# A one-token decode block on one Trainium2 core: how the output weight wo is laid out, loaded and multiplied at the end

## The chip, the cores and the metric

The kernel runs on one core of a Trainium2 chip. The metric is the time on the device of one execution in microseconds (us); the number of the kernel before is the median of ten executions. The profile is of one further execution with the hardware profiler on.

## The reference, cut to what matters

One token of width 512 is normalised and goes through an attention over a long cache and, beside it, a small two-layer network; both are added to the token.

```python
xn = _layernorm(x)                                  # x: (1, 1, 512), bfloat16
q = (xn @ wq) -> 32 heads of 128                    # wq: 512 x 4096
k, v = k_cache, v_cache, each head used by 4 q heads    # (1, 8, 65536, 128)
p = softmax(q k^T * 128 ** -0.5)
o = p v                                             # 32 heads of 128
A = o.reshape(1, 1, 4096) @ wo                      # wo: 4096 x 512
B = gelu(xn @ w1 + b1) @ w2 + b2                    # w1: 512 x 1792
return x + A + B
```

The cache is two times 134 MB, so nearly all of the 280 MB that are read are K and V. The weight wo has 4 MB; its row 128 h + d belongs to element d of head h.

## The kernel before, in words

**Tiling.** Eight groups (G) of four query heads (HPG) share a K and V head each. The 65,536 keys of a group are cut into four chunks, so there are 32 units of 16,384 keys. Two units make a pair, and `body(i)` works through pair i, 16 times. All of K, V and the weights of the first stage go through one SBUF tile, `kv`, of four slots of 4 MB (32 KB in each of 128 partitions): slots 0 and 1 take the K of even and odd units, slots 2 and 3 together the V of a pair.

**A body.** For each unit, `transposes` turns 128 x 128 blocks of K on TensorE (L585) into PSUM, VectorE and ScalarE copy them to `kt_ring` (L593, L595), and `scores` multiplies them by q (L605). `stats_1` and `stats_2` find the maximum and take exponentials; `pv` multiplies them by V (L676), 128 matmuls per unit, and VectorE keeps the result in `o_all` (L685). In the last body `weigh_1`, `weigh_2` and `weigh_3(0, GE, "oT")` weigh the chunks of the first seven groups (GE = 7) together into `oT_all`, which has d on partitions and one column per head; `weigh_3(GE, G, "oL")` does it for the last group after the last `pv`.

**What sets the order.** Each engine runs its own list, written out by hand. `_Sched.op` and `_Sched.dma` note what each step reads and writes and put semaphore waits where another engine or a DMA is to be waited for. All large loads are issued by SP, in the order of the list `chunks`: K of two units, V of the pair, and so on, at the end "W", which calls `dma_wo`. `issue_chunks` runs this list as slots come free; SP itself waits in that order, for a K slot till its transposes are done, for a V slot till its `pv` is done. When a pair of V has landed, GpSimd writes a one-element `flag` (L437), and the `pv` of the odd unit waits for that. PE, VectorE and ScalarE run the first 15 bodies or all 16 as a rolled loop.

**The end.** `dma_wo` loads wo for groups 0 to 3 and 4 to 6 in two DMAs of 4 KB rows into slot 0 (L469): for each group, partition p holds the four wo rows 4p to 4p + 3. The four heads of the last group go to slot 1 in 1 KB rows (L478): three heads in one DMA, the fourth in one of 120 partitions and one of 8. Since a partition of the first seven groups holds four neighbouring rows, the attention outputs must be moved to fit: sixteen small matmuls with columns of the identity (L774) pick them from `oT_all` into PSUM, and VectorE copies them to `oX_bf` (L778). Then `fin_mm` (L786) accumulates into one PSUM bank: 4 matmuls for the other branch and the bias (8 in the trace, as they are float32), 112 for the first seven groups, 16 for the last. VectorE copies the sum to `fin_bf` (L801), and SP writes it out (L805).

## Time and profile before

| | |
|---|---|
| median of ten executions | 659.0 us (658.77 to 659.18) |
| the profiled execution | 659.36 us |
| its span, first to last instruction | 657.6 us |
| mean TensorE clock granted | 0.768 of full speed |
| busy share: PE, DVE, ACT, POOL | 82%, 42%, 37%, 0% |
| read from HBM | 280.50 MB, 427 GB/s over the span |
| SP's queue | 9119 packets, 280.50 MB, 99.2% of 16 engines' span |
| instruction fetches (queue q8) | 8 packets, 0.13 MB |
| issue of the first wo load to its landing | 24.3 us for 2048 KB |
| issue of the second | 27.9 us for 1536 KB |
| three heads of the last group | 18.0 us for 384 KB |

How to read it: PE is TensorE, DVE VectorE, ACT ScalarE, POOL GpSimd; SP is the engine that only issues DMAs. A busy share is an average over the span; a wait for a DMA in it may be short and still set the end. The time from issue to landing of a load includes its time in the queue behind the loads issued earlier. The DMA share is that of the core's sixteen DMA engines, and the trace also keeps a record of each packet (a contiguous piece that one DMA engine moves): its start, its length, its bytes and its queue, though not its engine.

### The profile page before, as it was taken

What the parts mean: (1) busy time and instruction counts of PE and PEld (TensorE: products, weight loads), DVE (VectorE), ACT (ScalarE), POOL (GpSimd) and SP (SyncE); (2) the same over time, 40 slices, a digit from 0 to 9 for tenths busy, and PEclk for the clock granted to TensorE, in tenths of its full rate; (3) what the DMA queues carried; (4) which work ended last, traced back from release to release, by engine and by line L of the source; (5) the groups of instructions that cost most, each with busy time, mean ns of one, the idle gap of its engine ahead of it and who ended that gap; (6) DMA issues with size and microseconds to landing.
All of it is one profiled execution on the core that took longest, in us unless ns stands there. A gap on an engine that the chain in (4) does not pass through costs nothing.

```text
span 657.6 us, 27984 instructions
## 1 busy us (share of the span) xinstructions
PE 537.2 (82%) x12695; PEld 510.3 (78%) x12695; DVE 273.6 (42%) x565; ACT 245.0 (37%) x454; POOL 2.9 (0%) x27
## 2 busy tenths in 40 slices
PE   1388699988789697878969787895978879697897
PEld 0187698978788697868959787895978779597886
DVE  3145172725436162453516345261634526154352
ACT  0134162524425152352505335160443516144351
POOL 0000000000000000000000000000000000000000
PEclk9788596967869597786958778595877959588695
DMA  8999999999999999999999999999999999999997
GB/s 365 437 440 431 420 435 429 441 425 460 411 443 427 425 464 397 448 425 448 443 403 439 425 464 403 439 439 423 462 401 441 425 439 456 407 439 425 435 427 274
DMA packets 9277, 280.65 MB, mean 427 GB/s; under 512 B 1073, under 2 KB 1587, under 8 KB 2483
## 3 DMA queue, kind: packets, MB, share of 16 engines
q1 hardware_dynamic: 9119, 280.50, 99.2%
q8 instruction: 8, 0.13, 0.1%
q10 hardware_dynamic: 148, 0.01, 0.0%
q14 instruction: 2, 0.02, 0.0%
HBM read 280.50 MB, written 0.00 MB: 427 GB/s over the span
## 4 chain that ended last, share of the span: by engine, by line
DMA 65%; PE 32%; issue 2%; DVE 0%; SPq 0%
DMA kv<-in_A_k_cache_dram 61%; PE pst L585 25%; DMA kv<-in_A_wo_dram 4%; PE pss L605 4%; PE pO L676 2%; PE pA L632 0%; PE pss L786 0%; PE pA L643 0%; DVE pmax L613 0%; PE pA L692 0%; DVE gmax L634 0%; DVE diag L636 0%; SPq L460 0%; SPq L453 0%; SPq L457 0%
## 5 line engine op out<-in xcount | busy, mean ns | idle before, releaser
L595 ACT ACTIVATE kt_ring<-pst 128x1024 bf16<-128x1024 bf16 x192 | 195.6, 1027 | 311.1 <-PE pst L585 309.7
L585 PE MATMUL pst<-ident_bf,kv 128*128 128x128 bf16 x4096 | 282.1, 235 | 35.2 <-DMA kv<-in_A_k_cache_dram 35.1
L585 PEld LDWEIGHTS pst<-ident_bf,kv 128*128 128x128 bf16 x4096 | 263.8, 107 | 43.4 <-DMA kv<-in_A_k_cache_dram 36.6
L593 DVE COPY kt_ring<-pst 128x1024 bf16<-128x1024 bf16 x320 | 210.7, 687 | 121.6 <-PE pst L585 119.2
L676 PE MATMUL pO<-P_bf,kv 128*128 128x4 bf16 x4096 | 115.1, 166 | 38.5 <-DMA kv<-in_A_v_cache_dram 32.8
L676 PEld LDWEIGHTS pO<-P_bf,kv 128*128 128x128 bf16 x4096 | 113.6, 104 | 39.9 <-DMA kv<-in_A_v_cache_dram 34.0
L605 PE MATMUL pss<-q_cur,kt_ring 128*128 128x4 bf16 x4096 | 111.9, 164 | 3.8 <-issue 3.8
L605 PEld LDWEIGHTS pss<-q_cur,kt_ring 128*128 128x128 bf16 x4096 | 109.3, 96 | 3.9 <-issue 3.9
L654 ACT ACTIVATE P_bf<-pss,negm 128x128 bf16<-128x128 f32 x128 | 50.9, 548 | 67.5 <-DVE negm L646 67.5
L685 DVE COPY o_all<-pO 128x4 f32 (+1 forms) x32 | 5.2, 162 | 122.4 <-PE pO L676 122.4
L613 DVE TENSOR_REDUCE pmax<-pss 128x4 f32<-128x512 f32 x32 | 22.1, 692 | 67.6 <-PE pss L605 67.6
L654 ACT ACTIVATION_READ_ACCUMULATOR P_bf<-pss,negm 128x1 f32 x128 | 35.4, 277 | 0.0
L643 PEld LDWEIGHTS pA<-diag,ones_f 4*128 4x128 f32 x64 | 12.6, 245 | 18.2 <-DVE diag L636 16.5
L632 PE MATMUL pA<-ident_f,pmax 128*4 128x128 f32 x64 | 14.3, 312 | 12.5 <-DVE pmax L613 12.5
L643 PE MATMUL pA<-diag,ones_f 4*128 4x4 f32 x64 | 15.4, 309 | 10.0 <-DVE diag L636 10.0
L632 PEld LDWEIGHTS pA<-ident_f,pmax 128*4 128x4 f32 x64 | 2.9, 84 | 15.7 <-DVE pmax L613 14.0
L634 DVE TENSOR_REDUCE gmax<-pA 4x1 f32<-4x128 f32 x32 | 8.8, 274 | 9.5 <-PE pA L632 9.5
L668 DVE COPY sums_all<-sums 128x8 f32 (+1 forms) x16 | 2.7, 171 | 23.4 <-ACT P_bf L654 23.4
L692 PE MATMUL pA<-sums_all,ones_f 128*128 128x128 f32 x32 | 12.4, 491 | 0.0
L646 DVE TENSOR_SCALAR negm<-pA 128x4 f32<-128x4 f32 x32 | 5.1, 161 | 10.8 <-PE pA L643 10.8
L692 PEld LDWEIGHTS pA<-sums_all,ones_f 128*128 128x128 f32 x32 | 8.0, 312 | 0.0
L520 PE MATMUL pss<-kv,xnT_bf 128*1 128x512 bf16 x32 | 3.6, 627 | 4.8 <-DMA kv<-in_A_wq_dram 4.8
(75 smaller groups left out, 50.3 us busy)
## 6 DMA issues: line engine op xcount, KB each, us to landing
kv<-in_A_k_cache_dram SPq DMA_DIRECT2D x32, 4096.0 KB, 27.5
kv<-in_A_v_cache_dram SPq DMA_DIRECT2D x4, 4096.0 KB, 23.8
kv<-in_A_wq_dram SPq DMA_DIRECT2D x1, 4096.0 KB, 12.6
kv<-in_B_w_dram SPq DMA_DIRECT2D x2, 1792.0 KB, 18.3
kv<-in_A_wo_dram SPq DMA_DIRECT2D x1, 2048.0 KB, 24.3
kv<-in_A_wo_dram SPq DMA_DIRECT2D x1, 1536.0 KB, 27.9
kv<-in_A_wo_dram SPq DMA_DIRECT2D x1, 384.0 KB, 18.0
kv<-in_A_v_cache_dram SPq DMA_DIRECT2D x14, 31.1
```

Source lines behind the costliest of these rows:

```text
L585: lambda tb=tb, at=at, b=b, tt=s * TPB + t: pe.transpose(pst[tb][:, at * 128:(at + 1) * 128], slot[b][:, tt, :], ident_bf[:, :]),
L593: e, fn = DVE, lambda tb=tb, dst=dst: dve.tensor_copy(out=dst, in_=pst[tb][:, :])
L595: e, fn = ACT, lambda tb=tb, dst=dst: act.activation(out=dst, in_=pst[tb][:, :], func=ACTF.Copy)
L605: lambda k=k, kb=kb, at=at, t=t: pe.matmul(pss[k][:, at:at + HPG], lhsT=kt_ring[:, kb * BCOL + t * 128:kb * BCOL + (t + 1) * 128], rhs=q_c ...
L613: lambda k=k: dve.tensor_reduce(out=pmax[:, :], in_=pss[k][:, 0:CW].rearrange("p (t j) -> p j t", j=HPG), axis=AX.X, op=ALU.max),
L632: sch.op(PE, lambda: pe.matmul(pA[0:HPG, PA_ST:PA_ST + 128], lhsT=pmax[:, 0:HPG], rhs=ident_f[:, :], start=True, stop=True), reads=["pmax" ...
L634: sch.op(DVE, lambda: dve.tensor_reduce(out=gmax4[:, :], in_=pA[0:HPG, PA_ST:PA_ST + 128], axis=AX.X, op=ALU.max), reads=["pA"], writes=[" ...
L643: sch.op(PE, lambda: pe.matmul(pA[:, PA_SB:PA_SB + HPG], lhsT=ones_f[0:HPG, 0:128], rhs=diag4[0:HPG, 0:HPG], start=True, stop=True), reads ...
L654: lambda k=k, at=at, j=j, src=src: act.activation(out=P_v[k][:, :, j], in_=src[:, :, j], func=ACTF.Exp, bias=negm[:, at:at + 1], scale=1.0 ...
L676: lambda k=k, t=t: pe.matmul(pO[:, 0:HPG], lhsT=vslot[:, k * TPD + t, :], rhs=P_v[k][:, t, :], start=t == 0, stop=t == TPD - 1),
L685: sch.op(DVE, lambda: dve.tensor_copy(out=o_all[:, at_pair(i, PW, k * HPG, HPG)], in_=pO[:, 0:HPG]), reads=["pO"], writes=[f"o{k}"])
L692: sch.op(PE, lambda: pe.matmul(pA[:, PA_SUM:PA_SUM + NC], lhsT=ones_f[:, :], rhs=sums_all[:, :], start=True, stop=True), reads=["ones_f", ...
```

## The change

Of wo's first 28 heads (seven groups), what was two DMAs of 4 KB rows becomes three pieces, `WP`: four groups, two groups, one group. In a piece of n groups partition p holds 4n neighbouring rows of wo: 16, 8 and 4 KB. The first piece gets a buffer of its own, `wa`; the others stay in slot 0, and the 8 KB piece has the wait for that slot. The first piece is loaded in three parts. Partitions 0 to 111 are loaded by SP at the end, in place of the first wo load. Partitions 112 to 127 are loaded in sixteen DMAs of one partition from GpSimd's queue, each of 8,179 of the 8,192 elements, and a DMA of 16 x 13 elements by SP; both are placed ahead of body 4 (`dma_rest`), on GpSimd behind the flag of V pair 4. The fourth head of the last group is loaded in one DMA of 128 partitions.

The attention outputs are moved to fit in another way: for each piece, VectorE multiplies the columns of `oT_all`, repeated, by a mask of zeros and ones, `part_m` (`spread`, before the last `pv`), and one matmul with `part_r` sums the right rows. The two masks of each piece come from the identity by a reduction on VectorE ahead of the loop. Three matmuls replace sixteen; the copy to `oX_bf` comes ahead of `weigh_3(GE, G, "oL")`. The number of final matmuls is the same; the 64 of the first piece read `wa`.

```diff
--- before.py
+++ after.py
@@ -332,7 +332,21 @@
     w2_at = w1_at + KT * F
     w2_sb = kv[:, w2_at:w2_at + FC * D].rearrange("p (fc n) -> p fc n", fc=FC)
     GE = G - 1
-    wo_sb = kv[:, 0:GE * HPG * D].rearrange("p (g r n) -> p g r n", g=GE, r=HPG)
+    WP = []
+    g0 = 0
+    while g0 < GE:
+        n = next(m for m in (4, 2, 1) if g0 + m <= GE)
+        WP.append((g0, n))
+        g0 += n
+    NS = 16
+    WA = WP[0][1] * HPG
+    LP = WA * D - 13
+    wa = sb("wa", [128, WA * D], BF)
+    wo_sb = kv[:, WA * D:GE * HPG * D].rearrange("p (r n) -> p r n", n=D)
+
+    def wo_row(r, cols):
+        return wa[:, r * D + cols.start:r * D + cols.stop] if r < WA else wo_sb[:, r - WA, cols]
+
     wl_at = TPD * DH
     wl_sb = kv[:, wl_at:wl_at + HPG * D].rearrange("p (h n) -> p h n", h=HPG)
     kt_ring = sb("kt_ring", [128, NKT * BCOL], BF)
@@ -356,7 +370,10 @@
     rden = sb("rden", [128, H], F32)
     o_sum = sb("o_sum", [128, H], F32)
     oT_all = sb("oT_all", [128, H], BF)
-    oX_bf = sb("oX_bf", [128, HPG, GE], BF)
+    oX_bf = sb("oX_bf", [128, GE * HPG], BF)
+    oM_bf = sb("oM_bf", [128, len(WP), 128], BF)
+    part_m = [sb(f"part_m{i}", [128, DH // (n * HPG)], BF) for i, (_, n) in enumerate(WP)]
+    part_r = [sb(f"part_r{i}", [128, n * HPG], BF) for i, (_, n) in enumerate(WP)]
     flag = sb("flag", [1, 1], F32)
 
     pst = [nc.alloc_psum_tensor(f"pst{i}", [128, 1024], BF) for i in range(NPT)]
@@ -376,7 +393,9 @@
     sem_misc = sch.dsem("dmisc")
     sem_w1 = sch.dsem("dw1")
     sem_w2 = sch.dsem("dw2")
-    wsem = [sch.dsem(f"wsem{i}") for i in range(4)]
+    wsem = [sch.dsem(f"wsem{i}") for i in range(len(WP))]
+    lsem = [sch.dsem(f"lsem{i}") for i in range(2)]
+    sem_wa, sem_wb = sch.dsem("dwa"), sch.dsem("dwb")
     sem_vb = sch.dsem("dvb")
     sem_out = sch.dsem("dout")
 
@@ -460,26 +479,35 @@
         sch.dma(SP, lambda: sp.dma_start(out=w2_sb, in_=B_w2.rearrange("(p fc) n -> p fc n", fc=FC)),
                 sem_w2, writes=["w2"])
 
-    WG = (4, GE - 4)
     WH = (HPG - 1, 1)
 
+    def src_wa():
+        return A_wo[0:WA * DH, :].rearrange("(p r) n -> p (r n)", r=WA)
+
+    def dma_rest():
+        for p in range(128 - NS, 128):
+            sch.dma(POOL, lambda p=p: pool.dma_start(out=wa[p:p + 1, 0:LP], in_=src_wa()[p:p + 1, 0:LP]), sem_wa,
+                    writes=["wo0r"], total=16 * NS)
+        sch.dma(SP, lambda: sp.dma_start(out=wa[128 - NS:128, LP:WA * D],
+                                           in_=src_wa()[128 - NS:128, LP:WA * D]), sem_wb, writes=["wo0s"])
+
     def dma_wo():
-        g0 = 0
-        for i, n in enumerate(WG):
-            sch.dma(SP, lambda g0=g0, n=n: sp.dma_start(
-                out=wo_sb[:, g0:g0 + n].rearrange("p g r n -> p g (r n)"),
-                in_=A_wo[g0 * HPG * DH:(g0 + n) * HPG * DH, :].rearrange("(g p r) n -> p g (r n)", p=128, r=HPG)),
-                wsem[i], writes=[f"wo{i}"] + (["slot0"] if i == 0 else []))
-            g0 += n
+        for i, (g0, n) in enumerate(WP):
+            r = n * HPG
+            if i == 0:
+                sch.dma(SP, lambda: sp.dma_start(out=wa[0:128 - NS, :], in_=src_wa()[0:128 - NS, :]), wsem[i],
+                        writes=["wo0"])
+                continue
+            sch.dma(SP, lambda g0=g0, n=n, r=r: sp.dma_start(
+                out=wo_sb[:, g0 * HPG - WA:g0 * HPG - WA + r, :],
+                in_=A_wo[g0 * HPG * DH:(g0 + n) * HPG * DH, :].rearrange("(p r) n -> p r n", r=r)),
+                wsem[i], writes=[f"wo{i}"] + (["slot0"] if i == 1 else []))
         h0 = 0
         for i, n in enumerate(WH):
-            cuts = ((0, 128),) if n > 1 else ((0, 120), (120, 128))
-            for j, (p0, p1) in enumerate(cuts):
-                sch.dma(SP, lambda h0=h0, n=n, p0=p0, p1=p1: sp.dma_start(
-                    out=wl_sb[p0:p1, h0:h0 + n, :],
-                    in_=A_wo[(H - HPG + h0) * DH:(H - HPG + h0 + n) * DH, :].rearrange(
-                        "(h p) n -> p h n", p=128)[p0:p1, :, :]),
-                    wsem[2 + i], writes=[f"wl{i}"] + (["slot1"] if i == 0 else []), total=16 * len(cuts))
+            sch.dma(SP, lambda h0=h0, n=n: sp.dma_start(
+                out=wl_sb[:, h0:h0 + n, :],
+                in_=A_wo[(H - HPG + h0) * DH:(H - HPG + h0 + n) * DH, :].rearrange("(h p) n -> p h n", p=128)),
+                lsem[i], writes=[f"wl{i}"] + (["slot1"] if i == 0 else []))
             h0 += n
 
     dma_small()
@@ -721,6 +749,16 @@
                reads=["o_sum", "rden"], writes=[res])
 
 
+    def spread():
+        for i, (g0, n) in enumerate(WP):
+            r, a = n * HPG, DH // (n * HPG)
+            sch.op(DVX, lambda g0=g0, n=n, i=i, r=r, a=a: dve.tensor_tensor(
+                out=oM_bf[:, i, :].rearrange("p (h a) -> p h a", a=a),
+                in0=oT_all[:, g0 * HPG:g0 * HPG + r].unsqueeze(2).to_broadcast([128, r, a]),
+                in1=part_m[i][:, :].unsqueeze(1).to_broadcast([128, r, a]), op=ALU.mult),
+                reads=["oT", f"part_m{i}"], writes=[f"oM{i}"])
+
+
     def body(i):
         last = i == NU // 2 - 1
         for b in range(2):
@@ -749,6 +787,7 @@
         if last:
             weigh_2()
             weigh_3(0, GE, "oT")
+            spread()
         pv(2 * i + 1)
 
     for t, res in ((pss[0], "pss0"), (pss[1], "pss1"), (pO, "pO"), (pA, "pA")):
@@ -759,25 +798,30 @@
     ffn()
     free.add("V1")
     done_chunk("V0")
+    for i, (_, n) in enumerate(WP):
+        r = n * HPG
+        for t, res, pat in ((part_m[i], f"part_m{i}", "p (a r) -> p a r"), (part_r[i], f"part_r{i}", "p (a r) -> p r a")):
+            sch.op(DVE, lambda t=t, pat=pat, r=r: dve.tensor_reduce(
+                out=t[:, :], in_=ident_f[:, :].rearrange(pat, r=r), axis=AX.X, op=ALU.max),
+                reads=["ident_f"], writes=[res])
     marks, marks2 = [], []
     for i in range(NU // 2):
         marks.append(len(PE.ops))
         marks2.append((len(DVE.ops), len(ACT.ops)))
         assert not (DVE.pending or ACT.pending)
+        if i == 4:
+            dma_rest()
         body(i)
     marks.append(len(PE.ops))
 
 
+    for i, (g0, n) in enumerate(WP):
+        r = n * HPG
+        sch.op(PE, lambda g0=g0, i=i, r=r: pe.matmul(
+            pA[:, PA_O + g0 * HPG:PA_O + g0 * HPG + r], lhsT=oM_bf[:, i, :], rhs=part_r[i][:, :], start=True, stop=True),
+            reads=[f"oM{i}", f"part_r{i}"], writes=["pA"])
+    sch.op(DVX, lambda: dve.tensor_copy(out=oX_bf[:, :], in_=pA[:, PA_O:PA_O + GE * HPG]), reads=["pA"], writes=["oX"])
     weigh_3(GE, G, "oL")
-    for r in range(HPG):
-        for h in range(HPG):
-            sch.op(PE, lambda r=r, h=h: pe.matmul(
-                pA[32 * h:32 * h + 32, PA_O + r * GE:PA_O + (r + 1) * GE], lhsT=ident_bf[:, r:128:HPG],
-                rhs=oT_all[:, h:GE * HPG:HPG], start=True, stop=True),
-                reads=["oT", "ident_bf"], writes=["pA"], publish=r == HPG - 1 and h == HPG - 1)
-    sch.op(DVX, lambda: dve.tensor_copy(
-        out=oX_bf[:, :, :], in_=pA[:, PA_O:PA_O + HPG * GE].rearrange("p (r g) -> p r g", r=HPG)),
-        reads=["pA"], writes=["oX"])
 
     R = 0
     pR = pss[R]
@@ -788,11 +832,11 @@
 
     for kt in range(KT):
         fin_mm(kt, ones_f[:, 0:1], f_rows[:, kt * 128:(kt + 1) * 128], ["f_rows", "ones_f"], True, False, kt == KT - 1)
-    for g in range(GE):
-        for r in range(HPG):
+    for i, (g0, n) in enumerate(WP):
+        for r in range(g0 * HPG, (g0 + n) * HPG):
             for kt in range(KT):
-                fin_mm(kt, oX_bf[:, r, g:g + 1], wo_sb[:, g, r, kt * 128:(kt + 1) * 128],
-                       ["oX", f"wo{0 if g < WG[0] else 1}"], False, False, r == HPG - 1 and kt == KT - 1)
+                fin_mm(kt, oX_bf[:, r:r + 1], wo_row(r, slice(kt * 128, (kt + 1) * 128)), ["oX", f"wo{i}"] + ["wo0r", "wo0s"] * (i == 0), False, False,
+                       r == (g0 + n) * HPG - 1 and kt == KT - 1)
     for h in range(HPG):
         for kt in range(KT):
             fin_mm(kt, oT_all[:, GE * HPG + h:GE * HPG + h + 1], wl_sb[:, h, kt * 128:(kt + 1) * 128],
```

## The prediction

> **What bounds the kernel now.** I read the DMA share by stage, then the chain of waits in the last 34 us, then the packet records of the trace. The share first. After the clock and before GB/s, each row gives the share of the sixteen DMA engines that is busy.

> ```profile
> 100.00:200.00 100.00, 88.12 (x2155) 85.07 (x2153) 42.02 (x87) 38.81 (x71) 0.27 (x3) 0.76 1.01 434
> 200.00:300.00 100.00, 83.96 (x2011) 80.33 (x2009) 42.21 (x87) 39.20 (x78) 0.29 (x3) 0.77 1.00 432
> ...
> 500.00:600.00 100.00, 86.92 (x2051) 83.55 (x2049) 46.55 (x91) 43.64 (x76) 0.18 (x2) 0.80 1.00 434
> ```

> There is no idle DMA time, while PE is busy 84 to 88 us in 100. GpSimd's flag (L437), set when a pair of V has landed, shows the period: 38.65 to 38.83 us, 15 times. A period moves 16.8 MB, at 432 GB/s. So each nanosecond added to the busiest DMA engine, wherever it falls, is paid at the end, and one taken away is gained. The end:

> ```profile
> 624.92 0.39 SPq L469
> 625.31 0.04 issue
> 625.35 27.89 DMA kv<-in_A_wo_dram
> 653.24 0.04 issue
> 653.28 1.90 PE pss L786 x63
> 655.19 0.02 issue
> 655.21 0.29 DVE fin_bf L801
> ```

> The second wo load lands at 653.24, and 64 matmuls (48 of its own, 16 of the last group) follow. The last group isn't waited for, but is near: its 384 KB were issued at 636.28 and took 18.0 us (page, part 6), so 654.28; the 128 KB behind them add eight 1 KB packets per engine, starting 42 ns apart: about 654.6.

> In the packet records an engine takes 2,422 ns for 64 KB, 1,218 for 32 KB, 535 for 14 KB, 164 for 4 KB, 46 for 1 KB: about 14 ns a packet and 36.7 ns a thousand bytes. The sixteen counts of one K load arrive over 2.35 us; as no engine is ever idle, the late ones stay late to the end.

> One stretch of the tail matters most:

> ```profile
> 651.00:651.60 0.60, 0.59 (x24) 0.30 (x12) 0.00 (x0) 0.00 (x0) 0.00 (x0) 0.50 1.03 367
> 651.60:652.20 0.60, 0.00 (x0) 0.00 (x0) 0.00 (x0) 0.00 (x0) 0.00 (x0) 0.50 0.86 242
> 652.20:653.00 0.80, 0.00 (x0) 0.00 (x0) 0.00 (x0) 0.00 (x0) 0.00 (x0) 0.50 0.58 197
> 653.00:654.20 1.20, 0.92 (x38) 0.92 (x41) 0.00 (x0) 0.00 (x0) 0.00 (x0) 0.50 0.24 82
> ```

> Divide GB/s by share: 356, 281, 340, 342. From 651.6 to 652.2 a busy engine moves less than later, though later packets are the smallest. It is when the early engines reach the last load, the only one of 120 partitions. In it 4 KB packets of the late engines grow from 164 to as much as 239 ns and 1 KB packets from 46 to a mean of 70.

> [...] (4) [...] ACT's 28-byte packets come 1,215 ns apart, one after each 32 KB packet (1,213), and cost next to nothing.

> **The change, part by part.**

> Tail bytes. Before, an engine carries 56 packets of 4 KB, 56 × 164 = 9.18 us. After: 7 of 16 KB (by the fit 616 ns), 8 of 8 KB (315) and 8 of 4 KB (164): 4.31 + 2.52 + 1.31 = 8.14 us. So −1.04 us. The sixteenth row comes back earlier, at about 217 us, as one 16 KB packet per engine: +0.62. Net −0.42.

> Order at the end. The last piece before the final group is now 4 KB, and only 16 + 16 matmuls (0.94 us at 29.4 ns) follow it instead of 64 (1.88). Then the last landing decides: 654.6 − 0.42, four matmuls (0.12) and 0.05 to get going: 654.35 against 655.19, −0.84 with the bytes in it.

> Port conflicts in the 112-row load. [...] Lower bound zero (conflicts absorbed); [...] twice as long for all seven rows +4.3. The 120-row stretch showed factors of about 1.2 (4 KB mean) to 1.5 (1 KB mean). I take 1.4: 7 × 616 × 0.4 = +1.7.

> Port conflicts of the early rows. All sixteen lie in partitions 112–127, [...]: +2.0.

> Edits at nothing. Six reductions before the loop (nearest L699, 0.38 each, 2.3 in all) lie between VectorE's f_rows copy (ends 25.9) and its first kt_ring copy at 33.8, for which it waits 7.9. Uncovered they would cost 2.3. Three mask products (nearest L708, 0.29 each, 0.9) start at 647.2 and end before the second PV does at 648.7. Three matmuls replace sixteen (0.30 busy), and the oX copy moves ahead of weigh_3: oX comes some 0.4 earlier, oL 0.2 later, and both then wait for wo. The 112-row load has no slot to wait for, so SP issues it at about 613 instead of 624.9; the queue behind is full anyway. The 8 KB load keeps the wait for slot0 that L469 has. The 16 × 13 load is issued after V at 186.3, where SP idles till 198.3. The last load is whole again[...], so nothing. On GpSimd the flag of the next V (256.3) queues behind sixteen DMA issues that begin at 217.6, and the odd PV waits for that flag; each issue may take 2.4 us before it hurts. The trace shows no GpSimd DMA; [...] Uncovered at, say, 3 us each it would be 9 us late, once. Its packets and counts on another queue: nothing, after (4); each of sixteen counts on every engine at 9 ns would be 0.14.

> Sum: −0.84 + 1.7 + 2.0 = +2.9 us. The profiled execution took 659.36 (span 657.56, 1.80 around it), so 662.2; the median of ten is 0.36 lower: **661.9 us**.

> **Rivals.**
> Ports don't bind (0.14). For it: each stage moves the same bytes per partition, and the observed stretch is only 0.6 us of small packets. Against it: two packet sizes slowed together in it. Then only −0.84 is left, 658.2, not slower. It decides where both conflicts together cost under 0.84.
> One of the two conflicts acts (0.18): 659.0 − 0.84 + 1.7 = 659.9 or + 2.0 = 660.2.
> The early rows don't spread (0.06): sixteen rows on one engine are 9.9 us, 9.2 more than its share; an engine that is 2.35 ahead loses 6.9, a late one 9.2. With −0.84 and 1.7: 667 to 669.
> Both conflicts (0.62): 661.9, with their bounds from 659.4 [...] to 659.0 − 0.84 + 4.3 + 3.1 = 665.6.

> **Numbers.** Differences under about 0.2% (1.3 us) count as no change. The range, 658.1 to 665.6, takes in the first rival because it is the largest outside my case, and leaves out the last one and the ends. Faster by over 0.2% (under 657.7) needs the early rows to fall on early engines without conflict: 0.04. Within: most of the first rival and about half of the second, with the low end of my case: 0.22. Slower: 0.74.

> **What would show it.** Around 217 to 240 us K packets of some engines longer than 1,218 ns, and the flag period there longer than 38.8 by up to 3 us; packets of the 112-row load well over 616 ns; the sixteen counts of a K load spread wider than 2.35 us after the early rows; the last matmuls waiting for the last wo group, not for the piece before. If 16 KB packets take 616 ns throughout and the period stays, the port argument is wrong and the first rival holds. If GpSimd's flag comes late at 256, the queue is the cause.

## The result, and the profile after

The changed kernel takes 679.4 us (median of eight, 678.46 to 680.75) against 659.0 for the kernel before (28 executions, 658.77 to 659.32). The ratio is 1.0308, with a 95% interval of 1.0299 to 1.0317: 20.3 us slower, where 2.9 were forecast, and outside the range. The case that came true is the one to which the prediction gave 0.06, "the early rows don't spread", and it was dearer than its price there.

The page of the kernel after has these lines. The sixteen DMAs of GpSimd are issued in 8.3 us, and 280.65 MB at 414 GB/s stand against 280.50 MB at 427 before: the bytes are the same, and the stream is thinner.

```profile
span 677.9 us, 27986 instructions
...
DMA packets 9302, 280.65 MB, mean 414 GB/s; under 512 B 1610, under 2 KB 2124, under 8 KB 2252
...
q0 software_dynamic: 512, 0.26, 0.2%
...
L489 POOL DMA_DIRECT2D wa<-in_A_wo_dram x16 | 8.3, 526 | 0.5 <-issue 0.5
```

Where the time goes is read from GpSimd's flag, the clock of the stream: it is set when a pair of V has landed. This is GpSimd's timeline of the kernel after (start, duration; in brackets the idle time ahead of it, and what ended that).

```profile
217.19 0.09 POOL L456 MEMSET flag<- 1x1 f32 x1 [38.72 <-DMA kv<-in_A_v_cache_dram]
217.74 8.29 POOL L489 DMA_DIRECT2D wa<-in_A_wo_dram  x16 [0.46 <-issue]
266.02 0.09 POOL L456 MEMSET flag<- 1x1 f32 x1 [39.99 <-DMA kv<-in_A_v_cache_dram]
309.89 0.09 POOL L456 MEMSET flag<- 1x1 f32 x1 [43.78 <-DMA kv<-in_A_v_cache_dram]
348.64 0.09 POOL L456 MEMSET flag<- 1x1 f32 x1 [38.66 <-DMA kv<-in_A_v_cache_dram]
...
621.37 0.09 POOL L456 MEMSET flag<- 1x1 f32 x1 [38.69 <-DMA kv<-in_A_v_cache_dram]
665.54 0.09 POOL L456 MEMSET flag<- 1x1 f32 x1 [44.08 <-DMA kv<-in_A_v_cache_dram]
```

After a DMA group the brackets start at its end, so a period is read from the starts. 217.19 to 266.02 is 48.8 us and the next 43.9, where 38.8 is normal: 10.0 and 5.1 us are lost, 15.1 together. Then the periods are near normal for 311 us (about 1.1 us more is lost in eight of them), and the last one, 44.2, loses 5.4. So there are two losses and nothing of note between them: right behind the early rows, and in the tail.

The queue isn't the cause. GpSimd is free again at 226.03, 40 us before the flag it then sets. In the packet records the sixteen long packets of GpSimd's queue (16,358 bytes each) don't run side by side. They follow each other over 58 us, with 2.2 to 2.3 or 3.5 us from start to start while K comes in (32 KB packets) and 5.9 while V does (64 KB): one behind every one or two packets of the big stream, as on a single engine. The trace has sixteen counts for each K load, taken here to be one from each engine. Of those of the K load that lands from 264 us on, twelve arrive within 1.6 us of the first, three are 4.1 to 4.3 us late, and one 15.8; ahead of the early rows the last one was 1.94 late.

The end shows the same engine. Windows of the kernel after (us, busy of PE, PEld, DVE, ACT, POOL, then the granted clock, the DMA share and GB/s):

```profile
650.00:658.00 8.00, 6.59 (x179) 6.02 (x177) 3.80 (x8) 3.55 (x7) 0.00 (x0) 0.93 1.01 248
658.00:662.00 4.00, 3.96 (x127) 3.67 (x124) 1.30 (x6) 1.71 (x9) 0.00 (x0) 0.50 0.95 215
662.00:667.00 5.00, 1.22 (x46) 1.25 (x47) 2.37 (x9) 0.00 (x0) 0.09 (x1) 0.50 0.82 295
667.00:668.30 1.30, 1.30 (x55) 1.30 (x53) 0.00 (x0) 0.00 (x0) 0.00 (x0) 0.50 0.11 44
668.30:674.60 6.30, 5.16 (x168) 3.88 (x169) 0.71 (x5) 0.00 (x0) 0.00 (x0) 0.50 0.07 26
```

In the last row the share is 0.07 and the rate 26 GB/s: one engine in sixteen, at one engine's rate (427 GB/s over sixteen is 26.7). All the others are done. In the first two rows the engines are full, yet they move 248 and 215 GB/s: this is the second loss, treated below. The end of the chain of waits of the kernel after is the last landing, as the prediction's step on the order had it:

```profile
653.11 21.29 DMA kv<-in_A_wo_dram
674.40 0.14 issue
674.53 0.62 PE pss L830 x15
```

### The profile page after: what moved, and what is told of

Read it like the earlier page. It is cut to its first block, busy times and chain, and to the rows that moved or that the text cites. A ratio compares the mean times of both kernels' runs of the same rounds, so it can differ in the third digit from the quotient of the medians.

```text
span 677.9 us, 27986 instructions
## 1 busy us (share of the span) xinstructions
PE 539.4 (80%) x12682; PEld 511.7 (75%) x12682; DVE 275.7 (41%) x574; ACT 245.0 (36%) x454; POOL 11.2 (2%) x43
## 2 busy tenths in 40 slices
DMA packets 9302, 280.65 MB, mean 414 GB/s; under 512 B 1610, under 2 KB 2124, under 8 KB 2252
## 3 DMA queue, kind: packets, MB, share of 16 engines
HBM read 280.50 MB, written 0.00 MB: 414 GB/s over the span
## 4 chain that ended last, share of the span: by engine, by line
DMA 64%; PE 33%; issue 2%; DVE 0%; SPq 0%
DMA kv<-in_A_k_cache_dram 61%; PE pst L613 26%; PE pss L633 4%; DMA kv<-in_A_wo_dram 3%; PE pO L704 2%; PE pA L660 0%; PE pA L671 0%; DVE pmax L641 0%; PE pA L720 0%; PE pss L830 0%; DVE gmax L662 0%; DVE diag L664 0%; SPq L479 0%; SPq L476 0%; SPq L472 0%
## 5 line engine op out<-in xcount | busy, mean ns | idle before, releaser
L660 PEld LDWEIGHTS pA<-ident_f,pmax 128*4 128x4 f32 x64 | 2.9, 84 | 15.8 <-DVE pmax L641 14.0
L456 POOL MEMSET flag<- 1x1 f32 x16 | 1.4, 89 | 653.1 <-DMA kv<-in_A_v_cache_dram 653.1
L674 DVE TENSOR_SCALAR negm<-pA 128x4 f32<-128x4 f32 x32 | 5.1, 160 | 10.8 <-PE pA L671 10.8
L489 POOL DMA_DIRECT2D wa<-in_A_wo_dram x16 | 8.3, 526 | 0.5 <-issue 0.5
```

Source lines behind the costliest of these rows:

```text
L489: sch.dma(POOL, lambda p=p: pool.dma_start(out=wa[p:p + 1, 0:LP], in_=src_wa()[p:p + 1, 0:LP]), sem_wa, writes=["wo0r"], total=16 * NS)
L660: sch.op(PE, lambda: pe.matmul(pA[0:HPG, PA_ST:PA_ST + 128], lhsT=pmax[:, 0:HPG], rhs=ident_f[:, :], start=True, stop=True), reads=["pmax" ...
```

## The experiments

Two theories stood after this reading. *One engine*: all early rows are carried by a single DMA engine, which falls behind for good, and the packets of the tail's 112-row load hold each other up by where they write. The rival, *ports*: the early rows do spread, but all are written to partitions 112 to 127 and hold each other up there. "Port" is the author's name for a place where packets would crowd: the traces record none, and which partitions crowd is read from the times of the runs alone. Differences below are between medians; e1 is the base, since it has the new order and the mask products of the change without either suspect. The runs came in three sets; the kernel before had medians of 659.04, 658.98 and 659.11 us in them, so about 0.1 us of a difference between sets means nothing.

**e1: neither early rows nor a cut load.** The first piece is one load of 128 partitions at the end.

```diff
-  sp.dma_start(out=wa[0:128 - NS, :], in_=src_wa()[0:128 - NS, :]), wsem[i], writes=["wo0"]
+  sp.dma_start(out=wa[:, :], in_=src_wa()), wsem[i], writes=["wo0", "wo0r", "wo0s"]
...
-        if i == 4:
-            dma_rest()
```

> The first piece of wo comes in one load of 128 partitions at the end; no early rows, nothing on GpSimd's queue. Everything else as in the changed kernel. My theory now (two costs: all sixteen early rows on one DMA engine, and port conflicts of the load of 112 partitions): both are gone, so 658.2 us, 0.8 under the kernel before, with 16 KB packets of about 616 ns. Rival (the mask products, the three matmuls or the 16, 8 and 4 KB layout itself cost time): clearly over 660.

Measured: 658.45 us (21 executions), ratio 0.9991 [0.9985, 0.9998]. It is 0.6 us under the kernel before; the interval only just leaves out no difference. GpSimd's flags are 38.8 us apart, and the 16 KB packets at the end take 614.7 ns on average. Two of its flags, against which those of e2, e7, e9 and e10 are held, and the end of its chain of waits:

```profile
256.01 0.09 POOL L456 MEMSET flag<- 1x1 f32 x1 [38.69 <-DMA kv<-in_A_v_cache_dram]
294.79 0.09 POOL L456 MEMSET flag<- 1x1 f32 x1 [38.69 <-DMA kv<-in_A_v_cache_dram]
...
636.19 17.23 DMA kv<-in_A_wo_dram
653.42 0.14 issue
653.56 0.62 PE pss L828 x16
```

All 20.3 us and 0.6 more lie in the early rows and the 112-row load; the masks, the new order and the 16 KB rows together cost nothing.

**e2: the early rows alone.** Only the first of e1's two edits: the early rows are loaded as in the changed kernel, and again in the full load at the end.

> The early rows exactly as in the changed kernel, but the load at the end has all 128 partitions (it loads the sixteen rows a second time, so 0.26 MB more than before is read). One-engine theory: the flag periods around 217 to 310 us lose the same 15 to 16 us as in the changed kernel, the tail is clean: about 674. If the tail conflict were the larger part: under 668. If GpSimd's DMAs cost by delaying GpSimd's own queue: flag periods late without a single late engine in the K landings.

Measured: 675.17 us, ratio 1.0244 [1.0229, 1.0260], 16.7 over e1. Two flags of e2, the later one 15.3 us behind that of e1, and its tail in windows, to be held against that of the changed kernel:

```profile
266.20 0.09 POOL L456 MEMSET flag<- 1x1 f32 x1 [40.14 <-DMA kv<-in_A_v_cache_dram]
310.13 0.09 POOL L456 MEMSET flag<- 1x1 f32 x1 [43.84 <-DMA kv<-in_A_v_cache_dram]
...
650.00:658.00 8.00, 6.58 (x179) 6.01 (x176) 3.80 (x8) 3.56 (x7) 0.00 (x0) 0.93 0.94 400
658.00:662.00 4.00, 4.00 (x136) 3.94 (x132) 1.31 (x6) 1.71 (x9) 0.09 (x1) 0.50 0.86 325
662.00:663.50 1.50, 1.50 (x63) 1.50 (x60) 1.39 (x5) 0.00 (x0) 0.00 (x0) 0.50 0.11 44
663.50:669.70 6.20, 5.67 (x193) 4.65 (x190) 1.71 (x10) 0.00 (x0) 0.00 (x0) 0.50 0.07 26
```

400 over a share of 0.94 is 426, where the changed kernel has 248 over 1.01: with 128 partitions the tail runs at full rate. But the lone engine at the end (0.07, 26 GB/s) is here as well. So it comes from the early rows and not from the cut load.

**e3: the cut load alone.** No early rows; partitions 0 to 111 and then 112 to 127 are loaded by SP at the end.

```diff
   sp.dma_start(out=wa[0:128 - NS, :], in_=src_wa()[0:128 - NS, :]), wsem[i], writes=["wo0"]
+  sp.dma_start(out=wa[128 - NS:128, :], in_=src_wa()[128 - NS:128, :]), sem_wb, writes=["wo0s"]
...
-        if i == 4:
-            dma_rest()
```

> No early rows; the sixteen rows come from SP right behind the 112 at the end. Port theory: the packets of the 112-partition load take about 1.1 us instead of 0.62, so seven of them cost 3.5 us more per engine, and the end comes 4 to 5 us later than with one load of 128 partitions: about 662 to 663. One-engine theory alone (no conflict cost in the tail): 658 to 659.

Measured: 665.45 us, ratio 1.0097 [1.0082, 1.0112], 7.0 over e1 and more than expected. Its second load, of sixteen rows, which the changed kernel hasn't got there, may have a part in that. The 16 KB packets take 1,193 ns on average, 1.94 times those of e1. Two windows of e3:

```profile
644.00:648.00 4.00, 3.40 (x107) 3.14 (x105) 2.45 (x10) 0.00 (x0) 0.09 (x1) 0.50 1.02 233
648.00:652.00 4.00, 2.27 (x74) 1.75 (x70) 0.81 (x6) 0.00 (x0) 0.00 (x0) 0.50 0.96 186
```

and the same stretches of e1:

```profile
644.00:648.00 4.00, 4.00 (x135) 3.94 (x133) 2.54 (x10) 0.00 (x0) 0.00 (x0) 0.50 0.98 416
648.00:652.00 4.00, 3.73 (x129) 3.07 (x126) 0.72 (x5) 0.00 (x0) 0.00 (x0) 0.50 0.97 379
```

The share is the same and the rate about half: the engines are occupied, but move less. Whether that goes with the partitions they write to is what e5 and e6 test.

**e4: the early rows in other pieces.** Whole rows of 8,192 elements instead of 8,179, each of which shows in the packet records as sixteen packets of 1 KB, and not as one of 16,358 bytes, so that the pieces of a row can go to several engines; the small load of SP is dropped, and the 112-row load stays.

```diff
-    LP = WA * D - 13
+    LP = WA * D
```

> The early rows have all 8,192 elements, so the small SP load is gone and each row is cut in sixteen pieces of 1 KB. One-engine theory: the pieces go to sixteen engines, no engine falls behind by more than some 3 us [...], and the tail conflict of the 112 partitions stays: 662 to 666. Rival (GpSimd's DMAs are slow as such, or the rows hold up K wherever they go): still near 679.

Measured: 668.6 us, ratio 1.0144 [1.0129, 1.0160]: 10.8 us under the changed kernel, though 2.6 over the upper end of what was expected. No count is late by 16 us now. Three are, by 4.2 to 4.5 us, and the other thirteen arrive within 2.6; ahead of the early rows the last one was 2.1 late. So all engines lost about 1.5 us (the first count is that much later than in e1), and three at least 2.1 to 2.4 more; which three, the records don't name. In the changed kernel three counts are as late, beside the one at 15.8. Of the 10.1 us over e1, 3.9 are there by the flag at 608.86 (605.00 in e1); 6.2 fall in the tail. Why the tail takes that much here is not explained.

**e7 and e8: half as many rows, and as many DMAs of two rows.** Both load their rows again at the end, like e2.

```diff
-        for p in range(128 - NS, 128):
+        for p in range(120, 128):                      # e7
+        for p in range(128 - NS, 128, 2):              # e8, with wa[p:p + 2, 0:LP]
```

> As e2 (load of 128 partitions at the end), but only eight single rows early from GpSimd, 8,179 elements each, and no small SP load. One-engine theory: half of what e2 lost over e1 (16.7 us), so 8.4 us over e1, 666.8, and one engine about 8 us behind in the K landings. If the rows went to consecutive engines with some other loss per engine: little more than e1, or a loss that is not in proportion.

> As e2, but the sixteen early rows come in eight GpSimd DMAs of two rows (8,179 elements each). If the starting engine does not move on from DMA to DMA: eight rows on each of two engines, 8 to 9 us over e1, 666 to 668, and two late engines in the K landings. If it does move on and e2 is special to single rows: the rows spread over all engines[...]: 2.5 to 4 us over e1, 661 to 662.5.

Measured: e7 665.32 us, ratio 1.0094 [1.0077, 1.0111], 6.9 over e1; e8 668.44, ratio 1.0143 [1.0126, 1.0160], 10.0 over e1 (its executions lie between 666.6 and 668.5, the profiled one at 666.59; why they differ is open). GpSimd's timeline of e7:

```profile
217.76 4.22 POOL L489 DMA_DIRECT2D wa<-in_A_wo_dram  x8 [0.46 <-issue]
262.81 0.09 POOL L456 MEMSET flag<- 1x1 f32 x1 [40.83 <-DMA kv<-in_A_v_cache_dram]
301.59 0.09 POOL L456 MEMSET flag<- 1x1 f32 x1 [38.69 <-DMA kv<-in_A_v_cache_dram]
```

**e9 and e10: one DMA of sixteen rows.** In e9 the early rows are one GpSimd DMA to partitions 112 to 127; in e10 to partitions 32, 36, ... 92. Both load all 128 partitions at the end.

```diff
-        for p in range(128 - NS, 128):
-            ... wa[p:p + 1, 0:LP], in_=src_wa()[p:p + 1, 0:LP]
+        pool.dma_start(out=wa[128 - NS:128, :], in_=src_wa()[128 - NS:128, :])     # e9
+        pool.dma_start(out=wa[32:96:4, :], in_=src_wa()[32:96:4, :])               # e10
```

> As e2 (load of 128 partitions at the end), but the sixteen early rows, partitions 112 to 127, come in a single GpSimd DMA of 16 x 8,192 elements, so one row for each of sixteen engines. Port theory: nothing piles up on one engine, [...] 2.5 to 3.5 us over e1, 661 to 662. If only the pile on one engine mattered: at most 1 us over e1, 659.4.

> As e9, but the sixteen rows are partitions 32, 36, ... 92[...]. The load at the end of all 128 partitions overwrites them. Port theory: each engine loses its own row only, 0.6 to 1.0 us: 659.1 to 659.5. If the early load costs by being GpSimd's, whatever the partitions: as e9.

Measured: e9 661.95 us, ratio 1.0044 [1.0030, 1.0058], 3.5 over e1; e10 659.02, ratio 0.9999 [0.9990, 1.0007], 0.57 over e1, which its interval does not separate from e1's. The packets of e10 take 613 to 615 ns each; those of e9 from 746 to 2,487, 1,818 on average. As many bytes, in one DMA of sixteen rows, at the same place in the queue: the 2.9 us between the two go with the partitions that are written. (The rows of wo that are read differ too, but in e1 all of them load at 611 to 624 ns.)

The number of e9 was expected, the way to it wasn't. No engine stands out: the sixteen counts of the next K arrive over 2.17 us, little more than before (1.99), but from 228.27 us on, where e1 has 224.97 and e10 225.41. All sixteen engines fell back alike: the K packet behind the early row takes 1,984 to 4,001 ns on every engine. In e10 it takes 1,213 to 1,221, as always. So the rows for partitions 112 to 127 hold up the engines that carry them, K packets included, and those for 32 to 92 don't. GpSimd's timeline of e9:

```profile
217.65 0.61 POOL L488 DMA_DIRECT2D wa<-in_A_wo_dram  x1 [0.44 <-issue]
259.61 0.09 POOL L456 MEMSET flag<- 1x1 f32 x1 [41.35 <-DMA kv<-in_A_v_cache_dram]
298.38 0.09 POOL L456 MEMSET flag<- 1x1 f32 x1 [38.68 <-DMA kv<-in_A_v_cache_dram]
```

and of e10, whose flag at 256.79 is 0.8 us after e1's:

```profile
217.91 0.61 POOL L488 DMA_DIRECT2D wa<-in_A_wo_dram  x1 [0.43 <-issue]
256.79 0.09 POOL L456 MEMSET flag<- 1x1 f32 x1 [38.27 <-DMA kv<-in_A_v_cache_dram]
```

**e5 and e6: which partitions a load may be cut into.** e1 with its 128-partition load cut in two or three:

```diff
+  for a, b in ((0, 64), (64, 128)):                # e5
+  for a, b in ((32, 96), (0, 32), (96, 128)):      # e6
+      sp.dma_start(out=wa[a:b, :], in_=src_wa()[a:b, :])
```

> As e1, but the 16 KB rows come in two loads of 64 partitions, 0 to 63 and 64 to 127. Port theory [...]: 16 KB packets of about 1.23 us, 8 x 0.62 = 4.9 us more than e1: about 663.4[...]. Rival (a load of fewer than 128 partitions costs by its descriptors or its order in HBM): packets long in e5 and in the 64-partition load of e6 alike.

> As e1, but the 16 KB rows come in three loads: partitions 32 to 95, then 0 to 31, then 96 to 127. The first has the same shape as the loads of e5, four rows per engine[...]. Port theory: its packets take about 0.62 us, those of the two small loads about 1.23 [...], 4 x 0.62 = 2.5 us more than e1: about 661. Rival as in e5: at least as slow as e5, about 663.4 or more.

Measured: e5 664.73 us, ratio 1.0093 [1.0076, 1.0109], 6.3 over e1; e6 662.59, ratio 1.0057 [1.0040, 1.0074], 4.1 over e1. They are 1.3 and 1.6 us over what was expected, with e6 the faster, as the port theory has it. The windows of e6:

```profile
640.00:644.00 4.00, 3.90 (x128) 3.88 (x129) 1.33 (x6) 1.71 (x9) 0.08 (x1) 0.50 0.97 406
644.00:648.00 4.00, 4.00 (x135) 3.94 (x132) 2.54 (x10) 0.00 (x0) 0.01 (x1) 0.50 0.99 248
```

While only partitions 32 to 95 are being loaded, the packets take 611 to 622 ns and the stream runs at 406 GB/s; with the two loads of 32 behind them they rise to between 0.87 and 1.21 us. In e5, 80 of the 128 packets take 1.13 to 1.25 us, in the first load as in the second. The first load of e6 and the two of e5 have 64 partitions each: 611 to 622 ns a packet for 32 to 95, mostly 1.13 to 1.25 us for 0 to 63 and for 64 to 127. So the time goes with the partitions that are written together, and not with the cut or the size of the load as such. What sets 32 to 95 apart no run shows; that they would be free was the author's estimate, which no trace had shown before.

**e11: the kernel before with its last load whole.**

```diff
-            cuts = ((0, 128),) if n > 1 else ((0, 120), (120, 128))
+            cuts = ((0, 128),)
```

> The kernel before with the last head of wo in one load of 128 partitions instead of 120 and 8, the one other edit of the loads in the change. My prediction put it at nothing. Port theory: the slow stretch at 651.6 us is gone, the 4 KB packets there stay near 164 ns, and the piece before lands up to 0.2 us earlier: 658.8 to 659.1. If the last engine had been spared by the 120: 0.2 to 0.4 us slower.

Measured: 658.91 us, ratio 0.9997 [0.9989, 1.0005], no difference beyond the interval. But the stretch from which the prediction inferred conflicts is mended. In the window of e11

```profile
651.60:652.20 0.60, 0.03 (x4) 0.00 (x0) 0.00 (x0) 0.00 (x0) 0.00 (x0) 0.50 0.89 304
```

304 over 0.89 is 342, near the stretches around it, where the kernel before has 281; the 4 KB packets there take 163 ns on average, not 195. (Each of the two windows holds an instruction fetch of 16 KB, 1,125 and 1,247 ns long; without it the figures are 358 and 294.) So the load cut at partition 120 was the cause of that slow stretch.

## Why the prediction was wrong, point by point

**The bound: right.** The DMA stream sets the time, and what one engine loses is paid at the end: e7's 6.8 us are lost at one flag, and 6.9 stand in its time.

**Early rows: the step that failed.** The prediction took the sixteen rows to come back as one packet per engine, +0.62 us, with +2.0 for where they are written. They cost 16.7 (e2 over e1), because one engine carries them all. That each one-row DMA of GpSimd goes to another engine than the one before was assumed: the kernel before has no such DMA, so its trace could not show it. The runs show the same engines again each time: sixteen rows, one late count (15.8 us, changed kernel), eight rows, one (8.4 us, e7), eight pairs, two (8.3 and 9.0 us, e8).

**The two prices for rows that do spread: the first right, the second in size.** e10 pays 0.57 for its sixteen rows in partitions 32 to 92, and e9 pays 3.5 in 112 to 127, against 2.6 taken and 3.7 as the upper bound. But the +2.0 in the 2.6, like the 3.1 in the bound, was the author's estimate, which rested on nothing that a trace had shown, so that the size agrees there is in part luck. In e9 all sixteen engines fall back alike; three engines that fall back behind the rest, by at least 2.1 to 2.4 us, are seen in e4.

**The price of one engine: also too low.** That rival counted 0.62 us per row. e2's flag at 310.13 is 15.3 us behind e1's at 294.79; with a lead of up to 1.9 us that the engine may have had, it lost 15.3 to 17.2 us on sixteen rows, about 1.0 each (0.85 to 1.1 from e7; a lead of 1.7 us would make it 1.06 in both). In the packet records a row takes about 0.75 us itself, and the packet behind it on that engine 1.51 to 1.63 us (32 KB) or 2.73 to 2.80 (64 KB) instead of 1.22 and 2.42, together 1.06 us a row. Taking turns with another queue doesn't cost that by itself: in e10 a row takes 0.61 us and the K packet behind it no more than usual. The rest goes with partitions 112 to 127 or with the one-row DMAs; no run separates the two. Sixteen packets that could fall on one engine, at even 0.62 us each, were the largest item on the table, and 0.06 of the chance was too little for it.

**The late engine stays late.** It regains something only where the others stand idle: from 310 to 349 us the DMA share is 0.91, and its lag on the first count falls from 14.8 to 10.0 us. This idle time is the price, not a relief: I read it as the fifteen waiting for a free slot, which the sixteenth holds up.

**The 112-row load: the direction right, the size wrong.** The prediction took a factor of 1.4 for seven packets, +1.7 us, with +4.3 as the upper end, an estimate from the stretch of the 120-partition load alone. Half of the 16 KB packets take between 1,051 and 1,185 ns in the changed kernel, a factor of 1.7 to 1.9, and the 8 KB packets behind them, not counted at all, have a median of 514 ns instead of 313. The changed kernel is 4.2 us over e2, which has one 16 KB row more per engine at the end: 4.8 like for like. It is paid by the late engine in an unforeseen place. That engine is still at V while the others load the 112 rows. Five of its last seven V packets take 2.0 to 2.4 us and one 1.5, instead of 1.22: 5.35 us in all, the 5.4 that the last flag period loses. Its own seven rows, when it comes to them, run alone at 611 to 619 ns. That the 112-row load holds it up fits e2, where the last load has all 128 partitions and no V packet of the tail takes over 1.25 us. Hence the last flag period of 44.2 us in the changed kernel, and 38.9 in e2.

**The sum of what was measured.** −0.6 (e1) + 16.7 (e2 over e1) + 4.2 (changed kernel over e2) = 20.3 us, the whole difference.

**The order at the end: right.** −0.84 was forecast, the 0.42 that the new packets save included. e1, which saves the same 0.42, gives −0.6 in the median and −1.0 in the span of the profiled execution; PE ends at 654.18 (654.35 forecast), behind the last landing and 16 matmuls. Some of it may come from the whole last load, which the prediction counted at nothing: e11 is 0.2 us under the kernel before of its set, which is not clear of the noise.

**The edits at nothing: right, with one estimate off.** In e1 they cost nothing that shows. Its timeline has the mask products (647.09 to 647.79), the matmuls and the copy where they were put, ahead of the landing of the last wo pieces:

```profile
648.73 0.19 DVE L821 CAST oX_bf<-pA 128x28 bf16<-128x28 f32 x1
...
651.18 1.02 PE L828 MATMUL pss<-kv,oX_bf 128*1 128x128 bf16 x32 [0.27 <-DMA kv<-in_A_wo_dram]
```

oX starts at 648.73, 0.75 us earlier than in the kernel before (0.4 forecast). Sixteen DMA issues on GpSimd take 8.3 us, 0.53 each, and end 40 us before the flag behind them is set, so they are hidden.

**What stays open.** Why GpSimd's DMAs don't move to another engine (the trace names no engine; that it is the same one is read from the single late count); why a row costs 1.0 us there and 0.6 in e10; e4's tail; e8's variation.

## What to carry to other kernels

Where the DMA stream is saturated, price a small DMA by the engine that ends up busiest and by the partitions it writes, not by its bytes: 0.26 MB cost 16.7 us as sixteen one-row DMAs to partitions 112 to 127, 3.5 as one DMA to the same partitions, and 0.6 as one DMA to partitions 32, 36, ... 92. Think twice before you cut a 128-partition load: none of the three cuts of the 16 KB rows was free (+4.1 to +7.0 us), and the cheapest one began with partitions 32 to 95, whose packets took 611 to 622 ns as long as nothing else of the piece was being loaded. And where a step rests on a placement that no trace has shown, work out the time for the worst placement first; if that is the largest number on the table, it belongs in the range.

## What was not expected of the hardware

The counts of a K load already arrive over 1.9 to 2.35 us before any early row. In the packet records of the kernel before, eight instruction fetches of 16 KB (queue q8, 0.13 MB) take 1.0 to 1.25 us of one DMA engine each, and a K packet of 1.7 us instead of 1.21 follows five of them: about 1.5 us lost by the engine that was hit. Seven of them fall between 28 and 83 us, and as no engine is idle for long afterwards, the spread lasts to the end. This is read from the records alone; no run took a fetch away.
